# Seven key transfers of a decode kernel, each issued as 112 rows and four pieces of four rows

## The chip, the cores and the metric

The kernel runs on one core of a Trainium2 chip. The time is device microseconds of that core; the figure used is the median of several executions, and the profile pages come from one more execution, which the hardware profiler records. Five engines work side by side: PE (matrix products and transposes; PEld is its weight load), DVE and ACT (elementwise work and copies), POOL (reductions over partitions) and SP, which here issues every data transfer. The transfers themselves are carried by 16 DMA engines.

## The reference

One token per batch row passes through two attention layers and two small feed-forward blocks. What matters here is the attention, with its two large caches (batch 8, 8 key heads, 4096 positions, 256 numbers each, in bfloat16, so 134 MB each):

```python
def _A_ref(x, k_cache, v_cache, wq, wo):
    q = (x @ wq).reshape(B, Sq, Hq, Dh).transpose(0, 2, 1, 3)   # 16 query heads
    k = jnp.repeat(k_cache, rep, axis=1)                        # 8 key heads, rep = 2
    v = jnp.repeat(v_cache, rep, axis=1)
    scores = jnp.einsum("bhqd,bhkd->bhqk", q, k) * (Dh ** -0.5)
    p = _softmax(scores, axis=-1)
    o = jnp.einsum("bhqk,bhkd->bhqd", p, v)
    return o.transpose(0, 2, 1, 3).reshape(B, Sq, Hq * Dh) @ wo

x = x + _A_ref(_layernorm(x), A_k_cache, A_v_cache, A_wq, A_wo)
x = x + _B_ref(_layernorm(x), B_w1, B_w2, B_w3, B_w4)
x = x + _A_ref(_layernorm(x), A_k_cache, A_v_cache, A_wq, A_wo)
x = x + _B_ref(_layernorm(x), B_w1, B_w2, B_w3, B_w4)
```

Both layers read the same caches, each needs all of them, and the core's own memory holds only a part.

## The kernel before, in words

For each batch row and key head there is a key tile and a value tile of 2 MB: 128 partitions with 16 KB each (32 positions of 512 bytes). A tile is four *units* of 512 KB, and the buffer `kv` has 30 slots of one unit each (`QUARTERS`). The first layer of row b + 1 and the second layer of row b are interleaved, so that some units stay in their slots and are used by both layers (`KEEP_K`, `KEEP_V`, `HOLD`).

`front` (keys) loads a key tile, transposes it piece by piece on PE in float32 pairs (`transpose_piece`, L1165), has DVE or ACT copy each piece back to `kv` (`evacuate`, L1148 and L1149), and multiplies it with the queries (L985). The softmax follows on DVE, POOL and ACT. `back` (values) loads a value tile and multiplies it with the probabilities (L1050), reduces the four partial sums (L1074) and applies its rows of `wo` (L1099). A unit's slot comes free when its last matrix product is done: L985 for keys, L1050 for values.

The order of all instructions comes from a planner. `Plan.schedule` walks through simulated time with a duration for every operation, chooses the next instruction of each engine, and for SP it decides in `next_kv` how many units go into one transfer (one to four, by the free slots that lie side by side) and when. It then calls `issue_kv` (from L605), which makes the transfer: `o.emit` writes it to SP's program, `o.dma` is the semaphore and the value at which it has landed, `o.dur` is what the planner believes that it takes. Each slot has a semaphore; a transfer of n units counts on that of its first slot, 16 for each transfer, and `slot_n[q]` is the number so far. `Plan.emit` writes each engine's instructions with their waits, and adds the increment to the last instruction that `emit` returned:

```python
            last = o.emit(eng)
            if o.dma is not None:
                last.then_inc(o.dma[0], 16)
```

The weights are loaded once at the start (`dma`, L599). Two of them, `wqx_sb` and `w3x_sb`, go in two transfers of 64 partitions each; nearly all else goes to 128 partitions at once.

Of the kernel before, what the change touches and what calls it, by code (L numbers as in the profile page):

```python
# [6 lines left out]
P = 128  # L7
# [13 lines left out]
KEEP_K = 5  # L21
KEEP_V = 6
HOLD = 2
MARGIN4, MARGIN2 = 6, 2
REP = 24
AT = (-4, -3, -2)
# [433 lines left out]
def bass_interleave_layers__gqa_block_cached__mixer_s_mlp__decode_kernel(  # L460
# [119 lines left out]
    slot_sem = [nc.alloc_semaphore(f"s_slot{i}") for i in range(QUARTERS)]  # L580
    slot_n = [0] * QUARTERS
# [24 lines left out]
                4 * at - 0.5, *row)  # L606

    loads = [0]

    def issue_kv(o, n, q):  # L610

        (cache, b, h), u = o.unit.tile, o.unit.u
        src = cache[b, h].rearrange("(m s) d -> m (s d)", m=P)[:, u * 2048:(u + n) * 2048]
        dst = kv[:, q * 2048:(q + n) * 2048]
        slot_n[q] += 1
        o.emit = lambda eng: eng.dma_start(dst, src)  # L616
        o.dma = (slot_sem[q], 16 * slot_n[q])
        o.dur = ((n << 15) / 26.88e3 + 8 * 0.008) / FASTER

# [318 lines left out]

    KEPT_K[HKV - 1] = range(4 - HOLD)
    KEPT_V = {HKV - 1 - i: range(max(4 * i + 4 - KEEP_V, 0), 4) for i in range((KEEP_V + 3) // 4)}  # L940
    done = {}

    def front(layer, b, h, prio=None):
# [21 lines left out]
        for u in banks_of:  # L965

            ks[u] = ks[u + HOLD - 4]
            back_in[u + HOLD - 4] = u
        held = {}
# [462 lines left out]
```

## Time and profile before

| | |
|---|---|
| median of 3 runs | 1109.37 us (1105.71 to 1112.99) |
| span of the profiled execution | 1109.5 us |
| PE busy | 971.3 us, 88% of the span |
| DVE, ACT, POOL busy | 573.0, 288.1 and 97.9 us |
| data moved | 441.13 MB, 398 GB/s in the mean |
| transfers issued by SP | 363, of which 72 key and 55 value transfers have 2 MB |
| instruction packets (queue q8) | 153 of 16 KB, 2.51 MB |

The profile shows each engine's busy time, the rate of the DMA engines in 40 slices of the span, the chain of work that ended last, and for each idle time of an engine what ended it. Beside the page, the trace gives the same for any stretch of time, the instructions in order, and single DMA packets with their start, duration and size, though not the number of the DMA engine. An engine's DMA work on a 2 MB transfer consists of eight packets of 16 KB (one for each partition's row) and one small packet that raises the semaphore. The span is the time from the first to the last instruction of that one execution.

### The profile page before, as it was taken

The page shows a single profiled execution, that of the slowest core. Times are in us where ns is not written, and L with a number is a line of the kernel's source. Part 1 is how long each engine was busy: PE and PEld are TensorE (multiplying, and loading weights), DVE is VectorE, ACT ScalarE, POOL GpSimd, SP SyncE. Part 2 cuts the span into 40 slices and gives each one's busy share as a digit, 9 for nine tenths or more (in the row PEclk, how much of TensorE's full clock was granted, in tenths as well). Part 3 has the DMA queues.
Part 4 walks back from the last instruction along what each step waited for, and adds up shares of the span by engine and source line. Part 5 has one row for each costly group of instructions (what it writes and reads, how often), then busy time and mean ns, then how long its engine had stood idle before and what let it go on. Part 6 is the DMA issues. An engine that isn't in the chain of part 4 may idle for free.

```text
span 1109.5 us, 42648 instructions
## 1 busy us (share of the span) xinstructions
PE 971.3 (88%) x19517; PEld 777.4 (70%) x19517; DVE 573.0 (52%) x1782; ACT 288.1 (26%) x844; POOL 97.9 (9%) x275
## 2 busy tenths in 40 slices
PE   4889889898889887999888898898889998899987
PEld 4678657786668756786667776777557886587774
DVE  4345445555455543655555554565445655366544
ACT  1133113331224301242122321234113330243120
POOL 0000010100100101010000100101010010101010
PEclk9899989989999969999898898999899997899898
DMA  9999999999999999999999989999999999999993
GB/s 332 410 424 421 389 388 424 425 421 380 412 424 424 418 344 428 422 425 418 378 424 423 421 326 381 425 424 420 387 402 424 425 410 364 420 423 407 329 399 163
DMA packets 54099, 441.13 MB, mean 398 GB/s; under 512 B 5776, under 2 KB 8992, under 8 KB 26528
## 3 DMA queue, kind: packets, MB, share of 16 engines
q1 hardware_dynamic: 53920, 438.41, 96.9%
q8 instruction: 153, 2.51, 0.9%
q14 instruction: 26, 0.21, 0.0%
HBM read 438.38 MB, written 0.01 MB: 395 GB/s over the span
## 4 chain that ended last, share of the span: by engine, by line
PE 54%; DMA 32%; SPq 4%; issue 4%; DVE 4%; ACT 1%; POOL 0%
PE psT L1165 20%; DMA kv<-in_A_k_cache_dram 20%; PE psM L985 15%; DMA kv<-in_A_v_cache_dram 12%; PE psP L1050 8%; SPq L616 4%; PE psR L1099 3%; PE psM L814 2%; PE psM L927 1%; PE psM L930 1%; DMA w3x_sb<-in_B_w_dram 1%; PE psP L1373 1%; PE psP L1074 1%; DVE oS L1066 1%; ACT pT L1019 1%
## 5 line engine op out<-in xcount | busy, mean ns | idle before, releaser
L1165 PE MATMUL psT<-ident_f,kv 128*128 128x128 f32 x2816 | 390.2, 284 | 23.3 <-DMA kv<-in_A_k_cache_dram 21.3
L1148 DVE COPY kv<-psT 128x512 f32<-128x512 f32 x415 | 284.3, 690 | 177.5 <-PE psT L1165 171.7
L1165 PEld LDWEIGHTS psT<-ident_f,kv 128*128 128x128 f32 x2816 | 313.2, 144 | 49.0 <-DMA kv<-in_A_k_cache_dram 28.3
L1149 ACT COPY kv<-psT 128x512 f32<-128x512 f32 x321 | 186.8, 586 | 385.4 <-PE psT L1165 384.9
L1050 PE MATMUL psP<-kv,pT 128*2 128x256 bf16 x4096 | 186.9, 292 | 27.8 <-issue 13.2
L985 PEld LDWEIGHTS psM<-q2T,kv 128*128 128x128 bf16 x4096 | 127.3, 99 | 48.0 <-issue 35.1
L985 PE MATMUL psM<-q2T,kv 128*128 128x48 bf16 x4096 | 142.5, 188 | 18.2 <-issue 14.4
L985 PEld LDWEIGHTS psM<-q1T,kv 128*128 128x128 bf16 x4096 | 135.1, 97 | 18.9 <-issue 12.5
L985 PE MATMUL psM<-q1T,kv 128*128 128x48 bf16 x4096 | 143.9, 184 | 2.2 <-issue 1.2
L1050 PEld LDWEIGHTS psP<-kv,pT 128*2 128x2 bf16 x4096 | 78.5, 84 | 70.2 <-issue 25.3
L1019 ACT ACTIVATE pT<-sS,nb,fac 128x32 bf16<-128x32 f32 x128 | 52.7, 417 | 244.0 <-DVE nb L1013 244.0
L1009 POOL PARTITION_ALL_REDUCE gm<-pm x128 | 45.6, 356 | 763.1 <-DVE pm L1007 718.0
L1004 DVE COPY sS<-psM 128x64 f32<-128x64 f32 x128 | 28.6, 223 | 108.4 <-PE psM L985 105.6
L1064 DVE CAST oS<-psP 128x256 bf16<-128x256 f32 x128 | 54.0, 422 | 49.3 <-PE psP L1050 46.9
L1099 PE MATMUL psR<-wo_sb,oT 128*1 128x448 bf16 x448 | 68.6, 390 | 4.2 <-DVE oT L1080 2.3
L1023 POOL PARTITION_ALL_REDUCE Db<-rs x128 | 51.1, 399 | 213.2 <-ACT pT L1019 213.2
L1074 PE MATMUL psP<-sel,oS 128*128 128x2 bf16 x512 | 32.1, 166 | 34.6 <-DVE oS L1066 31.1
L1074 PEld LDWEIGHTS psP<-sel,oS 128*128 128x128 bf16 x512 | 25.2, 99 | 52.5 <-DVE oS L1066 43.8
L1019 ACT ACTIVATE pT<-sS,nb 128x32 bf16<-128x32 f32 x128 | 40.9, 326 | 69.6 <-DVE nb L1013 69.5
L1066 DVE TENSOR_TENSOR oS<-psP,oS 128x256 bf16<-128x256 f32 x128 | 54.1, 423 | 3.5
L814 PEld LDWEIGHTS psM<-x2c,wq_sb 128*128 128x128 bf16 x768 | 30.5, 98 | 19.4 <-issue 6.9
L814 PE MATMUL psM<-x2c,wq_sb 128*128 128x24 bf16 x768 | 36.4, 184 | 6.2 <-issue 5.3
(157 smaller groups left out, 579.1 us busy)
## 6 DMA issues: line engine op xcount, KB each, us to landing
kv<-in_A_k_cache_dram SPq DMA_DIRECT2D x72, 2048.0 KB, 20.5
kv<-in_A_v_cache_dram SPq DMA_DIRECT2D x55, 2048.0 KB, 17.2
kv<-in_A_v_cache_dram SPq DMA_DIRECT2D x121, 512.0 KB, 7.5
kv<-in_A_v_cache_dram SPq DMA_DIRECT2D x54, 1024.0 KB, 10.6
kv<-in_A_k_cache_dram SPq DMA_DIRECT2D x23, 1024.0 KB, 12.6
kv<-in_A_v_cache_dram SPq DMA_DIRECT2D x5, 1536.0 KB, 10.9
kv<-in_A_k_cache_dram SPq DMA_DIRECT2D x12, 512.0 KB, 8.1
wo_sb<-in_A_wo_dram SPq DMA_DIRECT2D x1, 3584.0 KB, 45.4
```

Source lines behind the costliest of these rows:

```text
L814: last = t.matmul(bank[:, at + i * step:at + i * step + copies], w, r, start=(kc == 0), stop=(kc == 3))
L985: last = t.matmul(ps[:, SB + 2 * i:SB + 2 * i + 2 * REP], a[:, c:256:2], bcast(rhs(c), REP, 1), start=(c == 0), stop=(c == 1))
L1019: return a.activation(pT[nr][:, :, :].rearrange("p i j -> p j i")[:, jj, :], sview[:, jj, :], ACT.Exp, bias=nb[nm][:, jj:jj + 1], scale=sc ...
L1023: plan.op("pool", lambda gp: gp.partition_all_reduce(Db[nr][:, :], rs[nr][:, :], P, RO.add), 0.5, "sum", rd=[("rs", nr, 0), ("rs", nr, 1)] ...
L1050: last = t.matmul(ps[g4:g4 + 2, PV0:PV0 + DH], pT[nr][:, i, :], slot_ap(q, s * 256, 256), start=(i < 4), stop=(i >= 28), skip_group_check= ...
L1064: plan.op("dve", lambda v: v.tensor_copy(oS[:, 0, :], po), 0.36, "o", rd=[("pv", par, x) for x in range(4)], wr=["oS0"], banks=[bk], prio=hi)
L1066: plan.op("dve", lambda v: v.tensor_tensor(oS[:, 1, :], po, oS[:, 0, :], ALU.subtract), 0.36, "o", rd=["oS0"] + [("pv", par, x) for x in r ...
L1074: last = t.matmul(ps[:, PV1 + 2 * c:PV1 + 2 * c + 2], oS[:, w, c:DH:2], sel[:, :], start=(w == 0), stop=(w == 1))
L1099: last = t.matmul(psR[r:r + 1, 0:D], oT[no][:, i % 2, i // 2:i // 2 + 1], wo_sb[:, a:a + D], start=(k == 1 and i < 2), stop=(k == HKV - 1 ...
L1148: return e.tensor_copy(dst, psT[bank][:, :])
L1149: return e.copy(dst, psT[bank][:, :])
L1165: last = t.transpose(psT[bank][:, s * P:(s + 1) * P], src, ident_f[:, :])
```

## The change

`issue_kv` counts the units that it has issued. When a transfer of four units comes up and 100 units or more (50 MB) have gone since the last time, the count starts anew and this transfer is split: the partitions 0 to 111 go as one transfer, and the partitions 112 to 127 as four transfers of four partitions. All five count on the same semaphore, and `slot_n` grows by five, so that whoever waits for the tile waits for all of them. This happens seven times, each time with a key tile.

```diff
+SPLIT, EVERY = 4, 100
...
     loads = [0]
+    since = [0]
 
     def issue_kv(o, n, q):
 
         (cache, b, h), u = o.unit.tile, o.unit.u
         src = cache[b, h].rearrange("(m s) d -> m (s d)", m=P)[:, u * 2048:(u + n) * 2048]
         dst = kv[:, q * 2048:(q + n) * 2048]
-        slot_n[q] += 1
-        o.emit = lambda eng: eng.dma_start(dst, src)
+        since[0] += n
+        top = P
+        if n == 4 and since[0] >= EVERY:
+            since[0] = 0
+            top = P - 16
+        slot_n[q] += 1 + (P - top) // SPLIT
+
+        def go(eng):
+            last = eng.dma_start(dst[0:top, :], src[0:top, :])
+            for p in range(top, P, SPLIT):
+                last.then_inc(slot_sem[q], 16)
+                last = eng.dma_start(dst[p:p + SPLIT, :], src[p:p + SPLIT, :])
+            return last
+        o.emit = go
         o.dma = (slot_sem[q], 16 * slot_n[q])
         o.dur = ((n << 15) / 26.88e3 + 8 * 0.008) / FASTER
```

## The prediction

> **What bounds the kernel now.** I read the page first: its shares, the rate slices, the DMA queues and the chain that ended last.
>
> ```profile
> PE 971.3 (88%) x19517; PEld 777.4 (70%) x19517; DVE 573.0 (52%) x1782; ACT 288.1 (26%) x844; POOL 97.9 (9%) x275
> ...
> GB/s 332 410 424 421 389 388 424 425 421 380 412 424 424 418 344 428 422 425 418 378 424 423 421 326 381 425 424 420 387 402 424 425 410 364 420 423 407 329 399 163
> ...
> q1 hardware_dynamic: 53920, 438.41, 96.9%
> q8 instruction: 153, 2.51, 0.9%
> ...
> PE 54%; DMA 32%; SPq 4%; issue 4%; DVE 4%; ACT 1%; POOL 0%
> ...
> kv<-in_A_k_cache_dram SPq DMA_DIRECT2D x72, 2048.0 KB, 20.5
> ```
>
> PE is busy for 88%, but the rate slices tell more: two to four slices at 420 to 425 GB/s, then one or two at 326 to 390, once for each of the eight batch rows. In the flat slices the DMA engines move all they can; in the dips the program waits for PE's own chains. A 2 MB transfer lands 20.5 us after its issue although it takes 4.9 us to move (2.097 MB / 424 GB/s), so three or four are queued. To see which side ends last in a flat stretch I took the chain of waits inside one:
>
> ```profile
> 176.86 1.02 issue
> 178.20 21.90 DMA kv<-in_A_k_cache_dram
> 200.14 3.89 PE psT L1165 x20
> ```
>
> The key tile issued at 178.20 lands at 200.10, and its first transpose (L1165) starts at 200.14, so there PE waits for the transfer. I then set each key tile's landing beside its first transpose. At the head of a stretch the tiles land early (the one issued at 151.3 lands at 165.3 and is first used at 169.8); 15 to 35 us later the slack is 0.04 us. A stretch is bound by the DMA queue: what the queue loses, the stretch loses.
>
> Last I looked for places where the queue is full and yet slow:
>
> ```profile
> 20.50:26.50 6.00, 5.33 (x43) 4.24 (x40) 3.39 (x5) 2.93 (x5) 0.00 (x0) 1.00 1.03 264
> ...
> 116.00:123.00 7.00, 4.79 (x98) 2.95 (x97) 3.62 (x10) 1.02 (x5) 0.75 (x2) 1.00 1.04 337
> 163.00:245.00 82.00, 74.69 (x1314) 63.16 (x1314) 43.53 (x110) 24.86 (x68) 6.79 (x18) 0.92 1.01 424
> ```
>
> The last two columns are the share of time in which the 16 DMA engines had a packet in work, and the rate. In the first two windows the engines are fully occupied and move only 264 and 337 GB/s. These are the windows of wqx_sb and w3x_sb, the only loads that go to 64 partitions at a time. Against 424 GB/s they lose 6 x (1 - 264/424) = 2.26 us and 7 x (1 - 337/424) = 1.44 us. The packet records say the same: the 128 packets of 4,096 bytes of wqx_sb took 299 ns in the mean, where the median packet of that size elsewhere took 159 ns (1.9 times), and the 16,384-byte packets next to them took up to 1.2 us, not 614 ns.
>
> **The change, part by part.** The schedule is computed before the transfers are written out, and the edit leaves o.dur alone, so no engine's order moves. Seven transfers are split, each a full key tile at the head of a flat stretch (before, these landed at 165, 306, 439, 569, 705, 836 and 973 us). Each becomes one transfer of 112 rows of 16 KB and four of four rows.
>
> *SP.* 4 x 7 = 28 more issues. An issue at L616 has a median of 328 ns, 430 ns with the gap behind it, so 1.7 us per split. It lies beside SP's own waiting (469 us for L985, 374 us for L1050). The tightest place is here:
>
> ```profile
> 690.96 0.33 SPq L616 DMA_DIRECT2D kv<-in_A_k_cache_dram  x1
> 692.75 0.33 SPq L616 DMA_DIRECT2D kv<-in_A_v_cache_dram  x1
> ```
>
> The next issue comes 1.79 us later, and what it brings lands 17 us later behind a queue. Cost 0; without that cover it would be 7 x 1.7 = 12 us. No engine's instruction gets a new wait, only a higher count on the slot's semaphore.
>
> *The engines' work.* Before, an engine moves 8 rows of a tile: 8 x 0.614 = 4.91 us. After, each moves 7 of the 112 rows (4.30 us), which is 0.61 us less; four of them move four more rows, 2.46 us, in all 6.76 us, which is 1.84 us more. That is the floor, with no slowing.
>
> *The slowing.* [...] The nearest rows are wqx_sb and w3x_sb. If every packet of the four loaded engines takes 1.9 times as long, they need 6.76 x 1.87 = 12.6 us, 7.7 us more than now. The upper end: the 112 rows at that ratio (8.0 us), and the sixteen rows of the pieces, which four engines write into four neighbouring partitions at a time, one after the other at the rate of one engine (16 x 0.614 = 9.8 us): 17.8 us, 12.9 more. I take 7.7, the measured ratio, between 1.84 and 12.9. As a cross-check: wqx_sb's 0.5 MB lost 2.26 us of 16 engines, so 256 KB lose 1.13 us of 16, or 4.5 us if four engines bear it, and 1.84 + 4.5 = 6.4 us.
>
> [...]
>
> *What hides part of it.* The engines are not level. Followed packet by packet, each instruction packet (q8) holds up the engine it falls on by 1.55 us, and they go round eight of the sixteen. So the sixteen landings of a tile lie 1.8 us apart at the head of a stretch and 3.3 us apart at the first tile without slack. If the four are not the late ones, their first part costs nothing; I take half of the mean spread, 1.2 us. Net: 7.7 - 1.2 = 6.5 us per split. The head's slack of 4 to 7 us does not help, since the four engines stay behind until the queue runs dry at the end of the stretch, and tiles with 0.04 us follow in six of the seven stretches. In the seventh the smallest slack is 2.7 us.
>
> *Sum.* 6 x 6.5 + (6.5 - 2.7) = 42.8 us. The profiled execution has a span of 1109.5 us, level with the median of 1109.37 us of the runs shown (1105.71 to 1112.99), so 1109.4 + 42.8 = 1152 us. What is late next is the whole rest of a stretch: the key tiles, the slots that their scores (L985) release, SP's next issues, then the value pieces.
>
> **The rivals.**
> *Levelling works (not slower).* The loaded engines are ones that carry no instruction packets, packets do not slow each other, and the late engines, relieved by one row, set the landing: 0.61 us less per split, 7 x 0.61 = 4 us, 1105 us. For it: half of the engines are free of instruction packets, and 1.55 us times the 2.4 packets of a cycle is more than the 1.84 us added. Against: the two 64-partition windows. It decides if the four stay below the late ones, that is if the excess is under about 2.5 us.
> *No slowing, but the four were not ahead enough.* 1.84 - 1.2 = 0.6 us, seven times: 1114 us. Against it is the same evidence.
> *Pieces go one row at a time.* 12.9 - 1.2 = 11.7, times 7, less 2.7: 79 us, 1188 us. For it: four engines on four partitions is denser than wqx_sb's sixteen on 64. Against: engines that start 1 to 2 us apart need not meet in every row.
> *The pieces don't share four engines* but go to different ones, so that each has 8 rows again: without slowing nothing changes, 1109 us. Neither the diff nor this trace shows which engines are used.
>
> **How the numbers follow.** A measurement of this kernel can tell about 1% (11 us) from no change. Slowing near the measured ratio has 0.55 (1125 to 1170 us, its own range), row by row or worse 0.20, no slowing but a loss 0.08, levelling 0.13, different engines 0.04. The time is that of the first, 1152. The cases within 1% hold 0.08 + 0.04 and nearly all of levelling: 0.21; faster by over 1% gets 0.04, since even perfect levelling gives 4 us; slower 0.75. The range goes from the levelling case, 1106, to the row-by-row case, 1188.
>
> **What would show it.** In the profile after, the seven key tiles stand as 112x and 4x transfers, with 28 more issues. Right, if the rate falls under 400 GB/s with occupied engines for some 10 us around each of them, if the sixteen landings of the following tiles lie 6 to 10 us apart (now 1.8 to 3.6), and if PE's wait for key transfers at L1165 grows from 28 us by about 40 us. Wrong, if the rate stays at 424 across the split and the landings stay within 4 us: then packets don't slow each other and the time stays within 5 us of 1109. Wrong as well if the landings spread and the span does not follow: then the slack at the head counts after all.

## The result, and the profile after

The changed kernel takes 1168.03 us (median of 4 runs, 1165.05 to 1170.05); the kernel before, run beside it, 1111.18 us. The ratio is 1.0525 with a 95% interval of 1.0493 to 1.0557: 57 us slower, 8.1 us for each of the seven splits. The forecast was 1152 us within 1106 to 1188, slower. The profiled execution has a span of 1165.4 us, 55.9 us more than the one of before. One execution of those reported below (1182.27 us, four transfers of 32 partitions) was in a slower state, over 1.5% above the fastest of its kernel, and is left out of the figures.

The page of the changed kernel, the lines that answer to those shown of before, and from its list of transfers the seven split tiles:

```profile
PE 984.9 (85%) x19517; PEld 789.3 (68%) x19517; DVE 574.0 (49%) x1782; ACT 287.6 (25%) x844; POOL 97.8 (8%) x275
...
GB/s 338 411 422 418 371 306 421 426 421 358 334 414 425 408 345 294 424 425 410 389 310 424 418 358 395 312 425 413 392 366 323 425 384 388 381 356 414 339 408 151
...
q1 hardware_dynamic: 54032, 438.41, 97.1%
q8 instruction: 153, 2.51, 0.9%
...
PE 56%; DMA 28%; issue 7%; SPq 4%; DVE 4%; ACT 1%; POOL 0%
...
kv<-in_A_k_cache_dram SPq DMA_DIRECT2D x7, 1792.0 KB
...
kv<-in_A_k_cache_dram SPq DMA_DIRECT2D x28, 64.0 KB
```

The bytes are the same, and the DMA engines are as occupied as before (97.1% against 96.9%), but the dips have become deeper: where the rate fell to 326 to 390 GB/s, it now falls to 294 to 323 in most. PE is busy for 13.6 us longer, at a mean granted clock of 0.912 (0.930 before), and waits more. The lower clock is no rival for the whole: over the 39 executions of the kernel before that stand beside the experiments (granted clock 0.917 to 0.939), 0.01 of clock goes with about 2.4 us, so 0.02 would be some 5 of the 57 us, an estimate, and nothing shows whether the clock is a cause or a consequence here. In the chain, "issue" (PE waits for nothing that the profile shows) rose from 4% to 7%.

The same in stretches of 28 us, one for each split of the changed kernel (columns: the stretch, its length, busy time of PE, PEld, DVE, ACT and POOL, PE's clock, the share of time in which the DMA engines had a packet in work, GB/s):

```profile
152.00:180.00 28.00, 18.48 (x396) 13.30 (x393) 7.72 (x31) 4.50 (x18) 2.80 (x8) 0.79 1.02 311
300.00:328.00 28.00, 21.01 (x448) 16.77 (x444) 10.62 (x35) 6.75 (x22) 2.66 (x7) 0.94 1.02 325
442.00:470.00 28.00, 20.06 (x401) 15.63 (x402) 10.72 (x33) 5.54 (x17) 2.51 (x7) 0.88 1.01 287
579.00:607.00 28.00, 20.61 (x423) 16.05 (x424) 11.43 (x36) 4.96 (x16) 2.66 (x7) 0.91 1.01 305
721.00:749.00 28.00, 20.37 (x412) 15.95 (x411) 10.65 (x33) 5.79 (x21) 2.66 (x7) 0.88 1.01 303
862.00:890.00 28.00, 20.46 (x401) 16.14 (x397) 9.67 (x32) 5.54 (x18) 2.26 (x6) 0.88 1.01 269
1009.00:1037.00 28.00, 23.29 (x451) 19.01 (x448) 12.21 (x34) 8.69 (x23) 2.35 (x7) 0.96 1.02 319
```

And the first of them in the kernel before; the other six there have 421 to 426 GB/s:

```profile
152.00:180.00 28.00, 23.48 (x537) 17.57 (x534) 11.45 (x41) 6.06 (x21) 3.29 (x9) 0.94 1.01 424
```

Against 424 GB/s the seven stretches lose 28 x (1 - 311/424) = 7.5, then 6.5, 9.0, 7.9, 8.0, 10.2 and 6.9 us: 56.1 us. The span grew by 55.9. In the sum, what the queue lost the kernel lost. Single stretches differ: matched instruction by instruction, PE falls behind by 8.5, 8.2, 8.8, 4.4, 9.6, 8.4 and 7.4 us from each split to the next (from the seventh to the end), so the fourth hides a part and the fifth adds one.

Inside the first split, in the changed kernel, same columns:

```profile
150.00:158.00 8.00, 6.00 (x160) 4.07 (x157) 2.80 (x12) 1.39 (x7) 1.11 (x3) 1.00 1.02 421
158.00:168.00 10.00, 5.32 (x144) 3.63 (x144) 2.19 (x9) 1.32 (x7) 1.16 (x3) 0.85 1.07 244
168.00:174.00 6.00, 5.26 (x112) 3.65 (x110) 1.89 (x8) 0.38 (x2) 0.36 (x1) 0.69 0.95 202
174.00:200.00 26.00, 23.89 (x387) 19.44 (x386) 13.23 (x33) 7.67 (x22) 1.90 (x5) 0.87 1.01 425
```

From 158 to 168 us the 112 rows move, on all sixteen engines (sixteen landings lie between 166.3 and 169.0 us), and the 16 KB packets take about 1.17 us (the median), not 0.61. From 168 to 174 us come the pieces, beside the tiles behind them; their last landing is at 174.8 us. Then the rate is back at 425 at once.

### The profile page after: what moved, and what is told of

It is laid out like the page before. It is cut to its first block, busy times and chain, and to the rows that moved or that the text cites. A ratio compares the mean times of both kernels' runs of the same rounds, so it can differ in the third digit from the quotient of the medians.

```text
span 1165.4 us, 42676 instructions
## 1 busy us (share of the span) xinstructions
PE 984.9 (85%) x19517; PEld 789.3 (68%) x19517; DVE 574.0 (49%) x1782; ACT 287.6 (25%) x844; POOL 97.8 (8%) x275
## 3 DMA queue, kind: packets, MB, share of 16 engines
q1 hardware_dynamic: 54032, 438.41, 97.1%
## 4 chain that ended last, share of the span: by engine, by line
PE 56%; DMA 28%; issue 7%; SPq 4%; DVE 4%; ACT 1%; POOL 0%
PE psT L1179 22%; DMA kv<-in_A_k_cache_dram 19%; PE psM L999 15%; PE psP L1064 9%; DMA kv<-in_A_v_cache_dram 8%; SPq L625 4%; PE psR L1113 3%; PE psM L828 2%; PE psM L941 1%; PE psP L1088 1%; PE psM L944 1%; DVE oS L1080 1%; DVE oS L1078 1%; DMA w3x_sb<-in_B_w_dram 1%; PE psP L1387 1%
## 5 line engine op out<-in xcount | busy, mean ns | idle before, releaser
L1179 PE MATMUL psT<-ident_f,kv 128*128 128x128 f32 x2816 | 403.4, 290 | 40.6 <-DMA kv<-in_A_k_cache_dram 34.6
L1179 PEld LDWEIGHTS psT<-ident_f,kv 128*128 128x128 f32 x2816 | 323.3, 148 | 67.7 <-DMA kv<-in_A_k_cache_dram 40.9
L1064 PE MATMUL psP<-kv,pT 128*2 128x256 bf16 x4096 | 187.9, 293 | 43.2 <-issue 28.4
L1064 PEld LDWEIGHTS psP<-kv,pT 128*2 128x2 bf16 x4096 | 78.9, 84 | 85.5 <-issue 39.3
L1033 ACT ACTIVATE pT<-sS,nb 128x32 bf16<-128x32 f32 x128 | 40.9, 326 | 70.1 <-DVE nb L1027 70.1
```

The source lines that it names most:

```text
L1033: return a.activation(pT[nr][:, :, :].rearrange("p i j -> p j i")[:, jj, :], sview[:, jj, :], ACT.Exp, bias=nb[nm][:, jj:jj + 1], scale=sc ...
L1064: last = t.matmul(ps[g4:g4 + 2, PV0:PV0 + DH], pT[nr][:, i, :], slot_ap(q, s * 256, 256), start=(i < 4), stop=(i >= 28), skip_group_check= ...
L1179: last = t.transpose(psT[bank][:, s * P:(s + 1) * P], src, ident_f[:, :])
```

## The experiments

Three theories were set against each other. *P*, placement: every packet of a transfer that is not laid out as 128 partitions is slow, on whatever engine, and makes its neighbours slow. *C*, concentration: only the queue of the four engines that the prediction gave eleven rows counts. *I*, issues: the number of transfers and semaphore counts costs the time. Later ones concern where the loss is taken up. All kernels but the last two change the same seven tiles, most of them only in how a tile is cut. The loop that writes the cuts is

```diff
+        cuts = [...] if top < P else [(0, P)]
+        slot_n[q] += len(cuts)
 
         def go(eng):
-            last = eng.dma_start(dst[0:top, :], src[0:top, :])
-            ...
+            last = None
+            for a, z in cuts:
+                if last is not None:
+                    last.then_inc(slot_sem[q], 16)
+                last = eng.dma_start(dst[a:z, :], src[a:z, :])
             return last
```

**112 rows and one piece of sixteen.**

```diff
+        cuts = [(0, 112), (112, P)] if top < P else [(0, P)]
```

> The rows 112 to 127 go as one transfer of 16 partitions (16 engines, a row each) and not as four pieces of four; the 112 rows stay. Theory P (placement: every packet of a transfer that is not 128 rows slows down, on all engines): by the changed kernel's windows the 112 rows lose 10 x (1 - 244/424) = 4.2 us per split and the pieces 6 x (1 - 202/424) = 3.1 us; sixteen engines on sixteen partitions still lose 1 to 2 us, so 7 x 5.5 = 38 us, about 1149 us (1140 to 1158). Rival C (concentration: the loss is the queue of the four engines that get 11 rows instead of 8): no engine has more than 8 rows, so 1111 us, within 5 us.

1157.41 us against 1112.38: ratio 1.0417 (1.0374 to 1.0460), 45 us, 6.4 us per split. The time is inside P's range, near its upper end. If the sixteen rows go to sixteen engines, as was expected, no engine has more than eight rows, and four fifths of the loss are still there: C is then wrong as the main cause, and the 112 rows alone, below, say the same. Four pieces in place of one add 8.1 - 6.4 = 1.7 us per split.

**Five transfers, cut along the row.**

```diff
+        cuts = [(0, 4096)] + [(c, c + 1024) for c in range(4096, 8192, 1024)] ...
-                last = eng.dma_start(dst[a:z, :], src[a:z, :])
+                last = eng.dma_start(dst[:, a:z], src[:, a:z])
```

> The same seven tiles go as five transfers, but cut along the row: 128 partitions each, 8 KB and four times 2 KB of every partition's 16 KB. Five issues, five counts on the semaphore, and packets of 2 KB, as in the changed kernel or smaller. Theory P: no loss, 1111 to 1114 us. Rival I (the number of issues, packets and semaphore counts costs the time): near the changed kernel, 1150 to 1168 us. Rival C: 1111 us.

1111.47 against 1112.38 us, ratio 0.9992 (0.9968 to 1.0016). Its list of transfers shows the pieces, 4 x 7 of 256 KB:

```profile
kv<-in_A_k_cache_dram SPq DMA_DIRECT2D x28, 256.0 KB, 12.3
```

As many issues and counts as in the changed kernel, with smaller packets, cost nothing that can be measured. I is out.

**Two halves of 64 partitions.**

```diff
+        cuts = [(0, 64), (64, P)] if top < P else [(0, P)]
```

> The same seven tiles go as two transfers of 64 partitions; each engine has 8 rows again. Theory P: as wqx_sb (2.26 us lost for 0.5 MB), so 4 x 2.26 = 9 us per split, 7 x 9 = 63 us, 1174 us (1155 to 1185). Rival C: nothing, 1111 us. Rival I: two issues rather than five, a fifth of the loss or less, under 1125 us.

1162.48 us, ratio 1.0455 (1.0413 to 1.0496), 50 us, 7.2 us per split; below P's point, inside its range, and far from C and I. The stretch of the first split, same columns as above:

```profile
152.00:180.00 28.00, 20.66 (x425) 14.73 (x426) 8.62 (x32) 4.89 (x19) 2.65 (x7) 0.82 1.01 326
```

All that was done here is to cut a tile in two equal halves by partitions. Each 64-partition transfer of wqx_sb raised its semaphore sixteen times as it landed (22.7 to 25.3 us and 23.8 to 26.6 us of the kernel before), so eight rows for each engine is an estimate from that.

**Only the 112 rows.** The rows 112 to 127 of the seven tiles are not loaded.

```diff
+        cuts = [(0, 112)] if top < P else [(0, P)]
```

> Only the 112 rows are loaded; the rows 112 to 127 of the seven tiles are left out, and the scores use what lies in the slot. Theory P: 4.2 us lost per split less 0.6 us for 256 KB that are not moved, 7 x 3.6 = 25 us, 1136 us (1128 to 1145). Rival C: every engine has one row less, 7 x 0.61 = 4 us faster, 1107 us.

1145.69 us, ratio 1.0282 (1.0237 to 1.0328), 33 us slower although 1.8 MB less are moved. Per split 4.8 us, and 0.6 us more for the 256 KB that were saved: 5.4 us. C had asked for a gain. P is right in direction and too low: 4.2 us was read off the first split alone, and the time is just above its range (1128 to 1145 us).

```profile
152.00:180.00 28.00, 20.38 (x440) 14.60 (x437) 9.03 (x33) 5.28 (x19) 2.84 (x8) 0.88 1.02 348
```

**Only the pieces.** The 112 rows of the seven tiles are not loaded.

```diff
+        cuts = [(p, p + SPLIT) for p in range(112, P, SPLIT)] if top < P else [(0, P)]
```

> Of the seven tiles only the rows 112 to 127 are loaded, in four pieces of four; the 112 rows are left out, and the scores use what lies in the slot. That takes 1.835 MB, 4.3 us of the queue, out of each split tile. Theory P with pieces that share one partition group: packets of the pieces take four times 0.614 = 2.5 us, the four engines need 9.8 us and not 4.9, 7 x 4.9 = 34 us less the lead of the others, 1125 to 1145 us. If their packets take 1.9 times (1.17 us) as everywhere else: 4.7 us, level with now, 1105 to 1113 us. Without any slowing: 2.5 us of four engines for 4.9, 7 x 2.45 = 17 us faster, 1095 us.

1115.78 us against 1110.81, ratio 1.0041 (1.0013 to 1.0069). That is 0.7 us per split, although each leaves out 4.3 us of transfer: the 256 KB in pieces cost about 5 us, as much as the 1.8 MB of the 112 rows. The time lies outside all three ranges, nearest to the middle one, but not for its reason. In the 30 us behind each split 64 to 98 packets of 16 KB take over 0.75 us (2 to 6 in the same windows of the kernel before), in the mean 1.1 to 1.7 us, at most 2.3 us. Only sixteen of them can be the pieces, so packets of other transfers are slowed too.

```profile
152.00:180.00 28.00, 19.81 (x458) 14.34 (x447) 9.53 (x35) 5.00 (x19) 3.03 (x8) 0.88 1.02 359
```

Alone the two parts come to 5.4 + 5.0 us, together to 8.1; the pieces slow down less when the packets around them are slow already. That is only argued.

**Other rows of HBM, the same partitions.**

```diff
+            rows = cache[b].rearrange("h (m s) d -> (h m) (s d)", m=P)
+            first = h * P + (2 if h == 0 else -2)
+            src = rows[first:first + P, u * 2048:(u + n) * 2048]
```

> The seven tiles stay one transfer to 128 partitions, but each partition reads the row of HBM that lies two rows away (of the same or the head before), so that the engines read other rows than usual; the scores of these tiles are those of shifted keys. If the slowing lies where the packets are written (which partitions an engine writes beside the others): no loss, 1111 us. If it lies in which rows of HBM an engine reads: 1140 to 1168 us.

1111.89 us, ratio 1.0005 (0.9980 to 1.0031).

```profile
152.00:180.00 28.00, 22.58 (x530) 16.94 (x523) 10.62 (x38) 5.86 (x20) 3.11 (x9) 0.94 1.01 425
```

The rate stays at 425 GB/s. Shifting the rows that are read was harmless with 128 partitions as the destination, which points to the written side. It doesn't prove it: the shift is only by two rows, and reading in the pattern of 112 or 64 rows while writing 128 partitions wasn't tried.

**A quarter of each tile.** 12 KB of each partition go to 128 partitions, the last 4 KB in 112 and four pieces.

```diff
+            cuts = [(0, P, 0, 6144), (0, top, 6144, w)] + [(p, p + SPLIT, 6144, w) for p in range(top, P, SPLIT)]
```

> Of the seven tiles the first 12 KB of every partition go as one transfer to 128 partitions, and only the last 4 KB of each as 112 partitions and four pieces of four: 0.5 MB of the 2 MB are cut by partitions, with 4 KB packets, and there are six issues for a tile. Theory P, priced by bytes: a quarter of the 8.1 us per split, 2.0 us, 7 x 2.0 = 14 us, 1125 us (1120 to 1132). A price for each split whatever its size: near 1168 us.

1127.83 us against 1112.95, ratio 1.0134 (1.0071 to 1.0198): 14.9 us, 2.1 us per split. A quarter of the bytes, about a quarter of the price (the interval allows 1.1 to 3.1 us): for a cut of this shape the price goes by the bytes, and not by the split.

**Four transfers of 32 partitions.**

```diff
+        cuts = [(p, p + 32) for p in range(0, P, 32)] if top < P else [(0, P)]
```

> The seven tiles go as four transfers of 32 partitions; each of 16 engines has two rows of each, eight in all. If the slowing goes by how many engines write into the same partitions (half as many partitions as with 64 + 64 for the same 16 engines): up to twice the loss of 64 + 64, 14 us per split, about 1210 us. [...]

1162.91 us against 1112.95, ratio 1.0471 (1.0406 to 1.0536): 50 us by the medians and 52 by the ratio, 7.1 to 7.5 us per split; the interval overlaps that of the halves. Half as many partitions in each transfer do not double the loss, and the 1210 us of the expectation are excluded. Why the loss is no larger than with the halves, no run here shows.

**The splits late in the stretches.**

```diff
-    since = [0]
+    since = [40]
```

> The changed kernel with the counter started at 40 units: eight splits (one more, a value tile near the end, issued at 1056 us), and they fall late in the flat stretches (issued at 79, 219, 351, 483, 617, 759 and 880 us of the kernel before) and not at their heads. Theory Q (the DMA queue is the bound all through a stretch, so what it loses is lost wherever it happens): 8 us each, 8 x 8 = 64 us, 1175 us (1160 to 1182). Rival F (the loss comes from PE, whose instruction packets are held up by the slow ones at the head of a stretch, where PE works off its program fastest): less than half, under 1145 us.

1176.37 against 1110.81 us, ratio 1.0585 (1.0545 to 1.0624): 65.6 us for eight splits, 8.2 us each. Within the noise (60.6 to 69.3 us by the interval) the place in the stretch does not matter. Theory F, that the loss needs PE's hurry at the head, is wrong.

**Fifteen splits.**

```diff
-SPLIT, EVERY = 4, 100
+SPLIT, EVERY = 4, 48
```

> EVERY is 48, so that 15 tiles are split and not seven, at the heads and in the middle of the stretches, three of them value tiles. Theory Q: 15 x 8.1 = 122 us, 1233 us (1210 to 1245). Rival F: only the seven or eight at the heads count, 1168 to 1185 us.

1256.88 us, ratio 1.1315 (1.1266 to 1.1363): 146 us, 9.7 us per split, more than the straight line of 8.1 and above Q's range (1210 to 1245 us). F is excluded again. Why more splits cost more each was not settled; the granted clock of PE fell to 0.887 in this run, from 0.930 in the kernel before.

Together: the same issues cut along the row cost nothing (ratio 0.9992), and every cut by partitions that loads the whole tile costs time (ratios 1.0134 to 1.1315), whether the parts are equal or not. With the shape kept, the price goes by the bytes; across shapes it doesn't, since 256 KB in four-row pieces cost about as much as 1.8 MB in 112 rows. What inside the DMA engines, or on the way to the partitions, slows the packets, no run here shows.

## Why the prediction was right or wrong

**The bound: right.** The flat stretches are bound by the queue, and its loss (56.1 us) is in the sum the kernel's (55.9 us). The late splits (8.2 us each) show that this holds late in a stretch too.

**The price of a split: the size near, partly by luck, and the place wrong.** I priced an excess of 7.7 us on *four* engines, with the other twelve a row ahead. The traces show a loss of all sixteen: the tile after the first split begins to land 6.4 us later than before (174.85 against 168.48 us) and ends 9.2 us later (179.37 against 170.23). So the sixteen landings lie 3.9 to 5.5 us apart in the tiles behind the splits and not the 6 to 10 us that I named as the sign. The sum's four loaded engines, the same four for all four pieces with eleven rows each, are shown by no run, nor is which engine moves which row; in their place the runs showed that one piece of sixteen rows takes off only 1.7 of the 8.1 us. The cut at 112 alone costs 5.4 us. The middle sum had no such term, since it slowed only the packets of the four loaded engines; that its 7.7 us lies near the 8.1 measured is luck. A row that the prediction shows would have come near the price: wqx_sb lost 2.26 us for 0.524 MB; by bytes that is 2.26 x 2.097/0.524 = 9.0 us for a tile, 63 us, 1172 us. That is somewhat too much: the halves, cut as wqx_sb is, measured 7.2 us. I used that row for the 256 KB of the pieces, as a cross-check, and not for the 2 MB that the cut displaces. The quarter tile agrees with a price by bytes for one shape of cut. Two readings were off as well: packets beside wqx_sb took up to 1.43 us and not 1.2, and the sixteen landings of the first tile without slack (landed at 200.10 us) lay 2.2 us apart and not 3.3; those of the tile behind it did.

**What hides it: wrong, both terms.** I took off 1.2 us per split for the lead of the four engines and 2.7 us in the seventh stretch for slack. Where all engines are late there is no lead. In the seventh stretch PE was 48.1 us late in the 8 us before the split was issued and 55.5 us at the end: 7.4 us stayed, where the sum had 3.8. The stretch that did hide a part is the fourth (4.4 us stayed), which the sum counted in full. Without the two terms the sum would have been 7 x 7.7 = 54 us, 1163 us.

**PE's waits: the wrong sign named.** PEld's wait for key transfers at the transposes was to grow by about 40 us. It grew from 28.3 to 40.9 us. Three waits of PEld before:

```profile
PEld psT L1165 <- DMA kv<-in_A_k_cache_dram: 28.3, 23, 4.7
PEld psP L1050 <- issue: 25.3, 58, 2.8
...
PEld psT L1165 <- issue: 20.0, 59, 1.5
```

And of the changed kernel, where L1050 is L1064 and L1165 is L1179:

```profile
PEld psM L999 <- issue: 53.0, 135, 2.8
PEld psP L1088 <- DVE oS L1080: 44.5, 52, 1.3
PEld psT L1179 <- DMA kv<-in_A_k_cache_dram: 40.9, 23, 7.6
PEld psP L1064 <- issue: 39.3, 49, 5.0
PEld psT L1179 <- issue: 25.8, 62, 2.8
```

The last section says what a part of the waits on "issue" is. The lateness enters in many small waits, and one line of the table does not carry it.

**SP's cover: right.** The five issues of the first split run from 151.20 to 153.1 us and the next one starts at 156.28; the columns cut (ratio 0.9992) shows that issues are free here.

**The rivals.** Levelling and "no slowing" are excluded by every cut by partitions. The row-by-row case, which asked for 11.7 us per split, is too high (8.1), and in the kernel with the pieces alone the slow packets take 1.1 to 1.7 us in the mean where four rows in turn would need 4 x 0.614 = 2.5. That each piece runs on four engines is supported: in the first split the slot's semaphore is raised once behind the issue of each piece (152.11, 152.62, 152.90 and 153.25 us) and then 32 times on landing (166.34 to 174.79 us), sixteen for the 112 rows and four for each piece; the same counts come in all seven. Which four, no trace shows. (In the text above, `issue_kv` starts at L610, not L605.)

## What to carry to other kernels

On a full DMA queue, cut a transfer along the row of each partition, not by partitions: the first cost nothing here (ratio 0.9992), the second cost some 3 to 4 us for each megabyte so cut in most of these kernels, even in two equal halves. Before shifting work between DMA engines, look for windows in which the engines are occupied and the rate is low, and price the change by the bytes that go that way, from a window with a cut of the same shape where there is one. Where the queue never ran empty, tiles that land early hid little of a loss here.

## What the runs showed of the hardware that was not expected

PE waited, by all signs, for its own program. In the changed kernel, in the timeline of PEld:

```profile
161.84 0.10 PEld L1064 LDWEIGHTS psP<-kv,pT 128*2 128x2 bf16 x6
166.90 0.73 PEld L1064 LDWEIGHTS psP<-kv,pT 128*2 128x2 bf16 x18 [4.96 <-issue]
```

And the same place of the program in the kernel before:

```profile
161.44 0.10 PEld L1050 LDWEIGHTS psP<-kv,pT 128*2 128x2 bf16 x6
163.22 0.67 PEld L1050 LDWEIGHTS psP<-kv,pT 128*2 128x2 bf16 x18 [1.68 <-issue]
```

The stall falls within one group of products. Counted in PE's program, the stalls at 156.8, 162.2 and 173.5 us are exactly 256 instructions apart, and one 16 KB packet of q8 holds about that many (2,506,752 bytes for 39,354 PE instructions, 63.7 bytes each). At 162.2 us the packet started at 164.12, landed at 165.40, and PE went on at 166.90; before, 160.87, 161.97 and 163.21. In the kernel before, one of a tile's sixteen landings falls back by 1.55 us behind such a packet, so instruction packets share the engines with the data. The packet of the changed kernel starts 3.25 us later than that of before, among data packets of 1.17 us in place of 0.61; that these hold it up, and PE's program with it, is inferred from that. Stalls over 0.3 us at such boundaries went from 31 with 39.5 us to 42 with 70.2 us. With the late splits they are 36 with 53.6 us, at a loss that is no smaller, and with the pieces alone 38 with 60.1 us, in an execution no longer than before (1106.1 us, with 12.85 MB less to load). So these stalls look like one way in which the loss reaches PE, and not like its source.
